# Relus and squares shared out among three engines, some weighted sums in two 64-row phases, both order strings new

## The chip, the cores and the metric

The kernel runs on one core of a Trainium2 chip. The metric is the device time of one execution in microseconds; lower is better. TensorE (PE in the profile) does the matmuls, VectorE (DVE), ScalarE (ACT) and GpSimd (POOL) the elementwise work, SyncE (SP) and POOL start most DMAs.

## The reference

Two layers are computed one after the other for 8 batches of 3136 rows with 256 channels.

```python
scores = (1.0 / S) * np.matmul(z, z.transpose(0, 2, 1))       # z: 3136 x 64
x = u * np.matmul(np.maximum(scores, 0.0) ** 2, v)            # u, v: 3136 x 256
proj = x @ w_proj                                             # 256 x 768, three parts x1, x2, x3
x2_conv = np.fft.irfft(np.fft.rfft(x2, axis=1) * np.fft.rfft(filter_fft, axis=0), axis=1)
out = (x1 * x2_conv * x3) @ w_out
```

The first layer is an attention without softmax: every score is cut at zero and squared. The second one multiplies two projections of its input with a circular convolution of the third.

## The kernel before

The score matrix is symmetric, so a block of it that was squared once can serve twice: as it is, and turned. The 3136 columns of a batch go in seven chunks (CHUNKS, five of 512, one of 256, one of 320), and the rows in 25 tiles of 128. A unit is a pair of row tiles against one chunk. For each unit that is scored (512 in all),

- `score_mm` (L1640) multiplies `zT` by `zT` into one of three pairs of PSUM banks, `ps_s`. z has 64 channels, so these matmuls use 64 rows of the array: two run side by side on the two row halves, or four 64x64 ones when spectral work of that form is in the same stretch ("quarters");
- `relu` (L1870) evicts the scores with a Relu on ScalarE into an fp32 buffer `R_t`, of which there are three (L1873);
- `sq` (L1875) squares `R_t` into a bf16 buffer `A_t`, on ScalarE (L1880) or VectorE (L1882, one multiply of `R_t` by itself);
- `mirror` (L1778) sends the blocks that a later chunk can use through a transposing DMA on SP's queue into a mirror buffer `M_t` (L1805);
- `weigh` (L1700) multiplies `A_t` or a mirror block by the rows of v, `v_t`, with 128-row matmuls, and adds up over all tiles in two PSUM banks `ps_o`, one for each half of the 256 channels (dh).

When a chunk's sum is complete, VectorE multiplies it by u into `xT_t` (L1924), and three projections follow. Two of them make the gate (L1196); the third goes through the spectrum: a first transform (`dft1`), a store to and load from DRAM, a second transform out of 64-row matmuls (`forward`), multiplications with the filter's spectrum in bf16 on VectorE (L1288 for the two products, L1292 and L1293 for the sums), the inverse (`inverse`), again through DRAM, and the last transform with the gate (L1382) and the output projection (`add_end`).

POOL in this kernel starts the DMAs that load and cast u, v and z (L614, L633), and once a chunk copies one element of `xT_t` (L623, `tick`) so as to start them when the chunk is done.

Nothing of this is written in the order in which it runs. Each piece is a `Task` with dependencies, the buffers it takes and frees, and a cost for each engine that may do it. `Plan.go` (L350) goes through time and hands out the tasks; the order in which it does so is the order of each engine's instructions. Two strings steer it. ORDER names, letter by letter, what TensorE does next: S a unit's scores, W a unit's weighted sum, Q a group of spectral matmuls, A, B and Z the projections, transforms and ends. ENGINES gives the engine, letter by letter, to each task that more than one could do (a ScalarE, d VectorE, p POOL). The planner counts 0.096 us where TensorE changes between 64-row and 128-row matmuls.

It also knows a weighted sum in two phases (letters "w" and "v", `weigh_rows` at L1683). In the first, the upper 64 rows are added into one accumulator while the lower 64 rows are added into the other; in the second, they change places. Such matmuls have 64 rows, like the scores. Both phases write the same accumulator, from the two row halves, so `by_rows` (L1673) makes TensorE wait for its own last matmul of the other rows there. The string of before has neither letter; `by_rows` is used only for the last half tile of 64 rows (L1681), whose two halves go to the two accumulators.

Of the kernel before, what the change touches and what calls it, by code (L numbers as in the profile page):

```python
# [16 lines left out]
ALU = mybir.AluOpType  # L17
# [32 lines left out]
    "WWWWSSWWWSWBWBWBWSSSWAAWAASSWAAWASSWBBAWWSSSWWWBWBAWWBSSWAWBWAWSSSWWBBWBWBWBBSSABAWWWBWWBWAAASWAWWWA"  # L50
    "BWSSBWABAWSSABWABAQSSWAWQSWAWSQSWWWWABWBWQSWWAASAWAAWWQSSWABAWSSQWAWQQSWWWSSSWWWWWQSSWWAAWAWAWAQSAWB"
    "QSSWAWAWWQSQWWWWWWSWSWQAWAWWWASSWAWAAWSQSWWAWWASQWWSSWWAASSWWAWWAWSSWSSWWSSWWSSWWWWSSWWBWWWABWSSSWAA"
    "WAASSWBAWBSSBWBAWWSSSWWWWWWSSBAWWABWWAAWSSSWBWBBSBBWAAAWASSBWBSAWBWAWSSWBWBWBWWBAWAAWBWBASABASQBWWAA"
    "BWSQSWWWSSQWWWWWWQSSWWAAAWAWAAWQSSWAABWSSQWWABWSSQWWWWSSQWWWSSSWWWAAWWAAWQSQWAAQSWAWWAWSSQWWWSQWWWSW"
    "QSWWWAWWAAAWWASAWSQAWAWWQSWWSSWWAASSWWWWSSSWAWSSSWWWWWWSSWWWSSWWWBWBABWSSSWAWAAASSWAAWAASSWBBWWABWSS"
    "SWWWWWSSBAWWBWWAASSWABWAASSBWBBAWABAWSSSWBWWBWBWWWSSWWAABWASSWAAAWABWSSQWAWWSBWSQSWBBWBWWWBWWSSQWWAA"
    "AWWSQBAWASQAWBWABWSSQWAWBWQSSWWWWSQSWWWSQSWWWAAAWAAWSQSWAAWWQSSWWAWWWSQSWWWWQQSWWWWWAASQAWAWAAQSWAWA"
    "WWWWSSSWWWAAWAWSSSWWAWSSSWWSSWWWWSSSWWWWWBSBWBWWSSSWAWAASSWAAWBASSWABBWBWWSSSWWAWBAWBWSSABWBWAWBABWA"
    "AAWSSSWAWBSSAWBWWBBWBWAWSSSWWWWSSWAWAWAAAWSSSWABBWABWBBAWQSSWWBWWBWSSQWWWQSWAAWWWASAAWQSABWAWSQSWAWQ"
    "SSWWWWWQSSWWWWSQBWAAWWQSAAWAWQSSWASAWWQSSWWWQQSWWWWWSQWAWAWAWAWWAAWSSQWWAAWWQSSWWWWWSSWWSSWWASSWWSSS"  # L60
    "WWWAWWWWWSSWAAWWWSSWABWSSBAWAAWSSSWBBWSAAWAAWWASSWABWWBBWWBWWAWWSSAAWASSAWABWSSSWABWSSSWBBWWABBWWBWA"
    "BWWWSSSWWBAAWWASSAAAWSQSWBBBWSQSWWWBWWWAWBBWAWQSWBAWASSWWAWSQQWAAWSQSWBAAWWQSWWBWABWSQSWWWWSSQWWWAAW"
    "SQAAWQSAWAAWSQSWAWWSSQWWWWSQSWWWQSWWAWAWAWAAWWQSSWAAWWSSSWWWAWWSSAWWAAWSSWAWSSSWWSWWWSSWWWWWSSSWWBWW"
    "BWBAWSSSWAWASSWAAAWAAWSSSWWWWBWWBBWBWBSSWBAAWWSSSWWAABWSSSWBBWAWAWBBWSSWBWBWWSSSWWAAWWBWBAAWSSQWWWQS"
    "BBWWSQSWWBBWWWWSQSWWBAWWZAWSQSWBABWWSQWSSSWABWWQSQWWWWWBWSSSWAWAWAWQSQWAWWSSQWWQSSWWWWSSSWWWZWWZWWQW"
    "AWSQWQSAAWWWWSSSWWWAWWQSSWWWWWSSSWAWWWWWWAWWWZZAAZAAZZBBBZZBBBZZBBZZZZZZQBQBZBBBQQQQQQQQBQQQQQZQZZZZ"
# [3 lines left out]
ENGINES = (  # L70
    "aaddddddddaadddddaaaddddaaddadadadddaadaadaaadaaaadddddddddddaaddadaaadadaddaaadaaadaddaddadaaadddaa"
    "adadaaaaaaaaddadadddadadaddaddaddddddadadadaaaaddadddaaddadadaaadadddaaadddaaaaddadaddddadaddadddada"
    "aaadddaaaaaaaddddddaddadddaaadaaaaaadadaaaaadaadddddadaddaaaaaaddaaaaddddddddddaaadadaaadaaddddaddaa"
    "addaadaadaaadadadaddadaaaaaddddadadaddddadaadaddddaadddaaaaadaddadddddaadaaadaadaaddaadadaaddaddaada"
    "daaddadaadaaadaadaddddadddaddddaaaddaadaddadddddaddadddaaaaddadaaadaaadadaddddddadaddddaaddaddaaddad"
    "daaaaaaaaaaddadaddddaaadadaaaaadadaddaaaadaaaadaaadadadadaaaadadaadadddddadadadadadddaaaaaaddadadadd"
    "dadddaaadaadadadadddaaaaaddddadaddaddddadaaaaddddaaddaaaadaaadadddadaddadddaadaaaadadaaddaadaaaadaaa"
    "daadadaaaaadaaaddddddddddaaaaaddadddadddaddadadadadddaadddaaaaaaaaaadaaaadadddadadadddadaaaddaaaaaad"
    "adadddddddddaaadaadaaaadadaadadadaaddaaaaddaaaaaaaadadddaaaaddadaddddadadadadadadadadadadaaaadaaddaa"
    "dadddadaadaaaaadaadadddadadaddadddadddaadaddadadddddaaadaaaaadaddadaadaaadaadaddddaaadaaadaadaddaaaa"  # L80
    "daaaaaddaddadaadddddadddaddadddaaddaaddddaadaadddaddaaaaaddaaaadaadaddddadaddaaddaaddadddadaddddadad"
    "daaaadadaaaaaaaaaaaadddadadaaadadadddaaddaaaaaadaaddaadddadaadddaddaadddaaaadaaaaaaaadaaaaaaaadaaaaa"
    "daaaaaaaaaaaadadddaaaaa"
)
# [1933 lines left out]
```

## Time and profile before

| what | us |
|---|---|
| median of 3 runs | 977.86 |
| lowest and highest of them | 975.88, 980.27 |
| the profiled execution | 977.09 |
| its span, first to last instruction | 975.3 |
| TensorE busy in the span | 942.9 |
| ScalarE, VectorE, POOL busy | 859.5, 830.5, 201.0 |

The profile is of one execution. A row of a group gives line, engine and operation, what is written from what, then the count, the busy time and the mean duration of one in ns, and the idle time of the engine ahead of them with what ended it. A row of the view in order of time gives the start, the duration of a row of like instructions, and in brackets the idle time ahead. A row of the view by stretches gives the stretch and its length, then for PE, PEld (weight loads), DVE, ACT and POOL the busy time and count, then TensorE's granted clock, the DMAs' busy share and GB/s. A matmul's duration contains the way through the array, so that of one is longer than the time by which the next one follows. The granted clock was 0.997 over the span.

### The profile page before, as it was taken

The page shows a single profiled execution, that of the slowest core. Times are in us where ns is not written, and L with a number is a line of the kernel's source. Part 1 is how long each engine was busy: PE and PEld are TensorE (multiplying, and loading weights), DVE is VectorE, ACT ScalarE, POOL GpSimd, SP SyncE. Part 2 cuts the span into 40 slices and gives each one's busy share as a digit, 9 for nine tenths or more (in the row PEclk, how much of TensorE's full clock was granted, in tenths as well). Part 3 has the DMA queues.
Part 4 walks back from the last instruction along what each step waited for, and adds up shares of the span by engine and source line. Part 5 has one row for each costly group of instructions (what it writes and reads, how often), then busy time and mean ns, then how long its engine had stood idle before and what let it go on. Part 6 is the DMA issues. An engine that isn't in the chain of part 4 may idle for free.

```text
span 975.3 us, 19343 instructions
## 1 busy us (share of the span) xinstructions
PE 942.9 (97%) x6664; PEld 468.5 (48%) x6765; DVE 830.5 (85%) x1492; ACT 859.5 (88%) x1161; POOL 201.0 (21%) x426
## 2 busy tenths in 40 slices
PE   6999999999999999999999999999999999999986
PEld 2344544355544545445444465444545455544654
DVE  8875788999899987898978997799888998889896
ACT  6788898999789999899988999899989999899783
POOL 5142311222012311213111130113201322000031
PEclk9999999999999999999999999999999999999998
DMA  9899899968998788997799997998979977896677
GB/s 156 147 173 176 119 176 159 186 127 152 182 219 176 137 185 179 212 175 151 148 207 189 180 150 173 207 198 155 155 157 206 213 155 152 188 207 143 164 208 241
DMA packets 332403, 170.31 MB, mean 175 GB/s; under 512 B 242598, under 2 KB 307942, under 8 KB 332304
## 3 DMA queue, kind: packets, MB, share of 16 engines
q1 hardware_dynamic: 302496, 132.43, 63.3%
q0 software_dynamic: 29168, 35.13, 24.0%
q10 hardware_dynamic: 640, 1.51, 0.5%
q8 instruction: 53, 0.87, 0.4%
q14 instruction: 46, 0.38, 0.1%
HBM read 90.26 MB, written 53.35 MB: 147 GB/s over the span
## 4 chain that ended last, share of the span: by engine, by line
PE 89%; DVE 4%; ACT 2%; DMA 2%; issue 2%; SPq 0%; ACTq 0%; DVEq 0%
PE ps_o_t L540 51%; PE ps_s L540 36%; ACT R_t L1873 1%; DVE A_t L1882 1%; PE ps_o_t L1681 1%; DMA conv_in_t<-spec 1%; DMA spec_in_t<-spec 1%; DVE yT_t L1382 1%; DMA M2e_t<-A_t 1%; DVE xh L1288 1%; DVE R_t L1288 0%; ACT A_t L1880 0%; DVE gate_t L1196 0%; PE ps_s L543 0%; DVE xT_t L1924 0%
## 5 line engine op out<-in xcount | busy, mean ns | idle before, releaser
L1873 ACT ACTIVATE R_t<-ps_s 128x1024 f32<-128x1024 f32 (+4 forms) x512 | 467.1, 963 | 54.2 <-PE ps_s L540 50.9
L540 PE MATMUL ps_o_t<-A_t,v_t 128*128 128x512 bf16 (+2 forms) x1936 | 441.4, 354 | 10.8 <-issue 4.4
L540 PEld LDWEIGHTS <-v_t 128*128 128x128 bf16 x2706 | 242.8, 98 | 255.2 <-issue 76.9
L1882 DVE TENSOR_TENSOR A_t<-R_t 128x1024 bf16<-128x1024 f32 (+2 forms) x274 | 300.4, 1112 | 30.4 <-ACT R_t L1873 27.1
L1880 ACT ACTIVATE A_t<-R_t 128x1024 bf16<-128x1024 f32 (+4 forms) x222 | 222.3, 1019 | 1.9 <-DMA M2e_t<-A_t 0.9
L540 PE MATMUL ps_s<-zT_t 64*128 64x512 bf16 (+5 forms) x1418 | 161.9, 356 | 1.9 <-DVE zT_t L577 0.5
L623 POOL COPY tick<-xT_t 1x1 bf16<-1x1 bf16 x54 | 14.7, 272 | 688.3 <-DVE xT_t L1924 688.3
L540 PE MATMUL ps_s<-xT_t,wp 128*128 128x512 bf16 (+2 forms) x411 | 104.5, 352 | 1.1 <-DVE gate_t L1196 0.5
L1924 DVE SCALAR_TENSOR_TENSOR xT_t<-ps_o_t,uT_t 128x256 bf16<-128x256 f32 (+2 forms) x224 | 76.0, 382 | 23.1 <-PE ps_o_t L540 18.3
L540 PEld LDWEIGHTS <-zT_t 64*64 64x64 bf16 (+1 forms) x1451 | 50.8, 100 | 91.9 <-issue 77.9
L573 ACT ACTIVATE x_t<-ps_s 128x512 bf16<-128x512 f32 (+2 forms) x126 | 71.8, 587 | 16.5 <-PE ps_s L540 14.7
L1196 DVE TENSOR_TENSOR gate_t<-ps_s,x_t 128x256 bf16<-128x256 f32 (+2 forms) x212 | 71.4, 383 | 17.4 <-PE ps_s L540 12.9
L1288 DVE TENSOR_TENSOR xh<-xh,H 128x1024 bf16<-128x1024 bf16 x120 | 82.1, 684 | 2.7 <-ACT xh L573 1.3
L540 PE MATMUL ps_o_t<-M_t,v_t 128*128 128x512 bf16 (+2 forms) x352 | 81.7, 353 | 0.0
L1382 DVE TENSOR_TENSOR yT_t<-ps_s,gate_t 128x512 bf16<-128x512 f32 (+2 forms) x95 | 57.0, 623 | 12.0 <-PE ps_s L540 11.6
L577 DVE CAST x_t<-ps_s 128x512 bf16<-128x512 f32 (+2 forms) x85 | 52.2, 623 | 12.3 <-PE ps_s L540 6.5
L614 POOL DMA_DIRECT2D un_t<-in_u_dram x112 | 59.9, 557 | 7.6 <-issue 5.7
L540 PEld LDWEIGHTS <-wp 128*128 128x128 bf16 x448 | 41.8, 98 | 39.6 <-issue 7.3
L633 POOL DMA_DIRECT2D v_t<-in_v_dram x112 | 59.4, 555 | 5.2 <-issue 1.9
L540 PE MATMUL ps_s<-wp,xT_t 128*128 128x256 bf16 x396 | 58.0, 273 | 0.2
L540 PE MATMUL ps_s<-wo,yT_t 128*128 128x256 bf16 (+1 forms) x360 | 54.3, 273 | 0.3 <-DVE yT_t L1382 0.2
L577 DVE CAST xh<-ps_s 128x512 bf16<-128x512 f32 x64 | 42.5, 684 | 8.7 <-PE ps_s L540 8.7
(166 smaller groups left out, 871.5 us busy)
## 6 DMA issues: line engine op xcount, KB each, us to landing
out_dram<-ost_t SPq DMA_DIRECT2D x60, 256.0 KB
spec<-s_t SPq DMA_DIRECT2D x96, 128.0 KB
spec_in_t<-spec SPq DMA_DIRECT2D x56, 192.0 KB
spec<-gs_t SPq DMA_DIRECT2D x56, 192.0 KB
v_t<-in_v_dram POOLq DMA_DIRECT2D x80, 128.0 KB, 5.0
un_t<-in_u_dram POOLq DMA_DIRECT2D x80, 128.0 KB, 5.4
conv_in_t<-spec SPq DMA_DIRECT2D x34, 256.0 KB
out_dram<-ost_t SPq DMA_DIRECT2D x18, 128.0 KB
```

The lines of the kernel that those rows point to most:

```text
L540: wrote(nc.tensor.matmul(o, *args, **kw), o)
L573: got = nc.scalar.activation(out_, in_, AF.Copy)
L577: got = nc.vector.tensor_copy(out_, in_)
L614: nc.gpsimd.dma_start(out=t[ds(j * N1, N1), lo - t0 : hi - t0, :], in_=x[:, n2 : n2 + hi - lo, :])
L633: nc.gpsimd.dma_start(out=t[ds(j * N1, N1), ds(v_at(a), (b - a) * D)], in_=r[:, n2 + a - lo : n2 + b - lo, :].rearrange("p t d -> p (t d)"),)
L1196: got = nc.vector.tensor_tensor(g[:, ::-1] if h == 0 else g, p, x, ALU.mult)
L1288: nc.vector.tensor_tensor(x[:, 1 - i], x[:, 0], h, ALU.mult)
L1382: got = nc.vector.tensor_tensor(yb["y"][:, dh, 0:w], p, gates[b, c, dh][:, 0:w], ALU.mult)
L1873: has_read(nc.scalar.activation(blocks(box["R"], n, cw)[:rows], p, AF.Relu), p)
L1880: nc.scalar.activation(a, r, AF.Square)
L1882: nc.vector.tensor_tensor(a, r, r, ALU.mult)
L1924: nc.vector.scalar_tensor_tensor(x, f, inv_s2, ut, ALU.mult, ALU.mult)
```

## The change

The Relu becomes a task for ScalarE or VectorE, the square one for ScalarE, VectorE or POOL (not POOL in the first chunk of the first batch). POOL's squares and VectorE's bf16 instructions of the spectrum and of z's copies (`ports`) are planned so that they do not overlap. ORDER and ENGINES are new as a whole: 2303 letters for 2245 and 1746 for 1223. ORDER now has 58 "w" and 58 "v"; ENGINES has 204 "p". The unit's second phase must come ahead of the last weighted sum of its chunk (`seconds`), a mirror buffer counts each of its uses, and the first chunk's transposes are planned as landing 2 us later.

```diff
+def c_pool(n):
+    return 0.12 + n * 0.00173
...
+        self.port = {"DVE": 0.0, "POOL": 0.0}
...
+        if engine in task.ports:
+            self.port[engine] = end
...
+            if e in task.ports:
+                s = max(s, self.port["POOL" if e == "DVE" else "DVE"])
...
             w_ = on("DVE", lambda mul=mul: mul(0), cost, evs, prio=ZP)
+            w_.ports = ("DVE",)
             w_ = on("DVE", lambda mul=mul: mul(1), cost, [w_], prio=ZP, lat=ZL)
+            w_.ports = ("DVE",)
             z_ = w_ if final else on("DVE", add, 2 * c_dve2(2 * D), [w_], prio=ZP)
+            z_.ports = ("DVE",)
...
+            if k == len(plans[b, c]) - 1:
+                deps += [(x, ISSUED) for x in seconds.get((b, c), ())]
...
-            if last:
-                t.frees.append((made[0], 0))
+            if not last:
+                made[0].holders += 1
+            t.frees.append((made[0], 0))
...
-                [] if made else [m_pool(c, a).slots], moves=0.78 * len(ts) * cw / 512, late=LATE_TURN,
+                [] if made else [m_pool(c, a).slots], moves=0.78 * len(ts) * cw / 512, late=LATE_TURN + 2.0 * (b == c == 0),
...
-            def relu(un=un, rows=rows, n=n, cw=cw, box=box):
+            def relu(e, un=un, rows=rows, n=n, cw=cw, box=box):
                 box["R"] = R_p.tile()
                 p = blocks(live[un], n, cw)[:rows]
-                has_read(nc.scalar.activation(blocks(box["R"], n, cw)[:rows], p, AF.Relu), p)
+                r = blocks(box["R"], n, cw)[:rows]
+                if e == "ACT":
+                    has_read(nc.scalar.activation(r, p, AF.Relu), p)
+                else:
+                    has_read(nc.vector.tensor_single_scalar(r, p, 0.0, ALU.max), p)
...
-                    nc.vector.tensor_tensor(a, r, r, ALU.mult)
+                    (nc.vector if e == "DVE" else nc.gpsimd).tensor_tensor(a, r, r, ALU.mult)
...
-            r_ = on(
-                "ACT", relu, c_act(n * cw), [(st, -sum(costs[i + 1 :]) - extra)], [R_p.slots], prio=0
+            r_ = job(
+                None, relu, both(n * cw), [(st, -sum(costs[i + 1 :]) - extra)], [R_p.slots], prio=0
             )
...
-            how = {"DVE": c_dve(n * cw)} if (b, c) == (0, 0) and k > 1 else {"DVE": c_dve(n * cw), "ACT": c_act(n * cw) + 0.039}
+            how = {"DVE": c_dve(n * cw), "ACT": c_act(n * cw) + 0.039, "POOL": c_pool(n * cw)}
+            if (b, c) == (0, 0):
+                del how["POOL"]
             q_ = job(None, sq, how, [r_], [a_p.slots], prio=1)
+            q_.ports = ("POOL",)
```

More of the change, by code (lines that the diff above doesn't have):

```diff
@@ L50 @@
[L50 to L54, printed above, removed]
@@ new lines @@
+    "WSQSWWAAWWwSSSvwwwQSvSvQWAWAAAWSSvQWAWAWWAWWSQSWWWWSSSwWAWAQwQvQvwwSSSWWQvSvWAAWAAWWQSWAWAAWWSSSWWSQ"
+    "QWWWWwSwQSWAAWAQvvSQWWWAASSWWAWSSAWWSQwSWAvSQAAWWWQSSWAWWAWWWWWSQSWWWAAWWAAWQwSQAWSvSAAWAAAWWWWWSSSW"
+    "WWWSSSwwWASSWSvvwSSvSWWWAWWWBWWAWSSAWBWAWBWASSBWASSwWAAWSSSWBBWBWBWSSvSWBWAAWBWAWBBWAWBAWSSBWBWAABWS"
+    "SWSSWWSSBWBWBWWWAWAAWSSSWWWWAAASAAAWAWBWSSSWQSSWWAAWSQSWWWWAWWAWSSSWWWBBAWQQAAWSQwABBWWQSwwSQvvvQWWA"
+    "WWQSWWWWQSSWWAWASSwQWWSQSWWvQSSWBAWAAWAWBWWAAAWSSAWAWWAASQWAAWWSSWWSQSWWWAWWSQSWAWWWWWSSSWWSwSSWWWAA"
@@ new lines @@
+    "vSSWAWWWBWWWSSSWWWWBABWSSSWABSWAABWSSSWWBABWSSBBWABWABWWWAAAWBWAWSSWWWASSWBAAWBABSwSvSSWWABSSWABWABW"
+    "WAWSSAWBASWBAWWAWAwSSSWBABWQQSWBWAWQQSvWAAWWWSQWAWBSSWBWBAWAAWAWWWSSSWWWQSSWQSWWWWQQSWAWAAWAWAWSAWAW"
+    "QQSWAWWSQSWWSwQSWWABWSvSSWWBWWSQAWWAWWSSWWQSSwWAWAWSSvQSWAAWWAWWAAAWAWWWSSAAWWSSSWWAWAWSSSWWWWAWBWWS"
+    "SSWWBBWWBBAWSwSSvSWWAAWABASSWWBAWBSSWWABWAWWBSSBWAWSSWBWBWBWBSSWABAAWBSSwSWWWvSSAAWWABAWWBSSWBAWWAAW"
+    "SSSWWAWSSAWBABSQWAWWSQAAWWQQAWWWWSSSWWWWABWSSQWAWBAWAAAwQvSSWWWAWSSQWBWAQQWWWSQSWWWAWWQSSwWBAWWSSQWv"
@@ new lines @@
+    "SQWWAWSSWWWAWBWAWWAWAWSSQWAQSWAWWSSWAAWWQSSWWAAWWAWAWSSSwwwSSvvvSWWWSSAAWWWWWWASSWWWBAWSSSWWABAWAASS"
+    "WAASSWBBAWSSABWBWBWWBWBAWWAABWWWWSSSWBBWBWSSSWWBABWSSSWBAWBWASSWWWAWSSBWWWBWWSSSWABAWASwQvSQWAWABWAW"
+    "WWSSWAABWWAAAWWSQWAAWBWWSSSWABQwSQABWAAWSSQvWWAWWSSSWWAAWQQWWWWSQSWWSSWWAASQWSwQABWBWAWvQSQWWWWQSAWW"
+    "WWWAWSQWSSSWWWWWAAWAWSQWSSWWAWAWAWSSAAAWwSSSWAAWWSSvSWWWAAWSSWBAWWWBWWSSwSWBAWBWAASvSAAWSSSWWSSWABWW"
+    "AWAWBSSWWBBBWSSBWWWAAWSSSWBABWBBAWSABAWASSWAABWWWBAWBWWWAWWBAWAWSSSwWSSvQWWQSSWWAWWBAAWAWQSQWAWBWWBW"
@@ L68 @@
+    "BBB"
 )
 ENGINES = (
[L71 to L75, printed above, removed]
@@ L84 @@
+    "dddadadddaadadadaddapddapdpaaadadadadaaapdadadaaadddaapdaadapadapdpdpaaadaaadapaddaaaadaddpapdaaadaa"
+    "aapapaaaadpapdaadaaaaaaapapaadaadaaaaaddpaaddddaaaaapapaaaaaddpaaadapaadaaaddaadpadaddaddaaadadddaaa"
+    "adaaddddadaaddaadaaaaaaaaaadaadapdaapaaapdaapapaaaaaaaadaaaapdpaaapaadadadpaaddaaadaadaaaapddddapdda"
+    "papdaaddaapaadpaaaaapadaadaaaaadadpapaaapdddaaaapaaaaaadpaadpapapdadadadpaddddadaaadadpaaaadaaadaaad"
+    "aaaaaaaadaaadaaaaaaaaaaaddaaaadaaaaadadddaaada"
 )
@@ L1544, in go_z @@
                 d = on("DVE", dup, c_dve2(P * (t1 - t0)), [a], [zd_p.slots], prio=2)
+                d.ports = ("DVE",)
                 d.frees.append((a, 0))
@@ L1697, in weigh_rows @@
                     )
-    w_first, w_last = {}, {}
+    w_first, w_last, seconds = {}, {}, {}
     def weigh(un, dhs):
```

49 lines of the change are left out of this document (23 added, 26 removed).

## The prediction

> **What bounds the kernel now.** I read the busy line and the chain on the page first, then the busy time by stretches, then the rows of TensorE in order of time, then the groups.
>
> ```profile
> PE 942.9 (97%) x6664; PEld 468.5 (48%) x6765; DVE 830.5 (85%) x1492; ACT 859.5 (88%) x1161; POOL 201.0 (21%) x426
> ...
> PE 89%; DVE 4%; ACT 2%; DMA 2%; issue 2%; SPq 0%; ACTq 0%; DVEq 0%
> ```
>
> ```profile
> 0.00:30.00 30.00, 21.75 (x110) 8.13 (x112) 23.34 (x57) 20.84 (x28) 13.27 (x35) 1.00 1.10 161
> ...
> 400.00:500.00 100.00, 98.68 (x703) 48.70 (x714) 85.94 (x153) 93.73 (x125) 19.94 (x41) 1.00 0.87 168
> ...
> 940.00:975.30 35.30, 24.70 (x274) 15.74 (x267) 25.94 (x55) 17.74 (x35) 8.02 (x15) 0.92 0.75 224
> ```
>
> TensorE is busy for 98.7 of 100 us in the middle and holds 89% of the chain; it idles only in the first 30 us (8.3) and the last 35 (10.6). So a microsecond of gain must come out of TensorE's own stream or out of the two ends, and any wait put into that stream is paid in full. What that stream wastes is seen where it changes between 128-row matmuls and the 64-row ones of the scores and spectra:
>
> ```profile
> 452.57 1.04 PE L540 MATMUL ps_o_t<-A_t,v_t 128*128 128x256 bf16 x8
> 453.54 0.41 PE L540 MATMUL ps_s<-xh,TZ 64*64 64x512 bf16 x4
> 453.78 0.31 PE L540 MATMUL ps_s<-zT_t 64*64 64x320 bf16 x4
> 454.02 0.83 PE L540 MATMUL ps_o_t<-A_t,v_t 128*128 128x256 bf16 x6
> ...
> 464.47 0.99 PE L540 MATMUL ps_o_t<-A_t,v_t 128*128 128x320 bf16 x6
> 465.39 0.61 PE L540 MATMUL ps_s<-zT_t 64*128 64x512 bf16 x4
> 465.93 1.47 PE L540 MATMUL ps_o_t<-A_t,v_t 128*128 128x512 bf16 x5
> ...
> 467.46 0.59 PE L540 MATMUL ps_o_t<-A_t,v_t 128*128 128x512 bf16 x2
> ...
> 468.65 1.03 PE L540 MATMUL ps_o_t<-A_t,v_t 128*128 128x512 bf16 x4
> ```
>
> Two more 512-column matmuls take 0.44 us (x4 against x2), so one occupies 0.22 us, and by columns one of 256 takes 0.11 and one of 320 takes 0.135. Eight of 256 from 452.57 end at 453.45. Four 64x64 matmuls run side by side, so the next two rows are 0.22 + 0.135 of work; the stretch to 454.02 is 1.45 us for 1.23 of work. The 64-row stretch costs 0.22 us beyond its work. The second one: 1.46 us from 464.47 to 465.93, for 6 x 0.135 + 2 x 0.22 = 1.25 (two matmuls of 64x128 run side by side), 0.21 over. I take 0.215 us a stretch.
>
> **The change, part by part.** Counts are from the instruction order of the two built kernels. Durations are of the profiled execution, 977.09 us: a span of 975.3 and 1.8 around it, and 0.8 under the median of the three runs shown.
>
> *Order of TensorE.* Before, the 64-row matmuls lie in 275 stretches; after, in 248, since 58 of 928 weighted sums now run in two 64-row phases ("w", "v") inside a stretch of scores. Columns streamed stay the same. 27 x 0.215 = **-5.8 us**. The phases bring 427 more matmuls and weight loads; weight loads are 48% busy beside the matmuls, so I cost them at nothing. New is a wait of TensorE for itself, 70 times, when the rows change on the same accumulator. In the order, 54 of them have over 0.5 us of other matmuls in between and are covered; the other 16 have one or two steps of 0.22 us. No such wait is in the trace: between nothing and one such step, 0 to 16 x 0.22 = 3.5; I take **+1.5**, nearer to the middle, as nothing else is queued that could hide them.
>
> *The first 35 us.* A mirrored block's transpose is planned 2 us later for the first chunk.
>
> ```profile
> 29.60 1.23 DVE L1882 TENSOR_TENSOR A_t<-R_t 128x1024 bf16<-128x1024 f32 x1 [2.29 <-DMA M2e_t<-A_t]
> ...
> 31.63 0.59 PE L540 MATMUL ps_o_t<-A_t,v_t 128*128 128x512 bf16 x2 [1.96 <-DVE xT_t L1924]
> ```
>
> VectorE stood 2.29 us for that transpose, and TensorE then 1.96. Between 0 and -2.0; I take **-1.0**, since the same transposes still have to land.
>
> *Who does the elementwise work.*
>
> ```profile
> L1873 ACT ACTIVATE R_t<-ps_s 128x1024 f32<-128x1024 f32 (+4 forms) x512 | 467.1, 963 | 54.2 <-PE ps_s L540 50.9
> ...
> L1882 DVE TENSOR_TENSOR A_t<-R_t 128x1024 bf16<-128x1024 f32 (+2 forms) x274 | 300.4, 1112 | 30.4 <-ACT R_t L1873 27.1
> L1880 ACT ACTIVATE A_t<-R_t 128x1024 bf16<-128x1024 f32 (+4 forms) x222 | 222.3, 1019 | 1.9 <-DMA M2e_t<-A_t 0.9
> ...
> L573 ACT ACTIVATE x_t<-ps_s 128x512 bf16<-128x512 f32 (+2 forms) x126 | 71.8, 587 | 16.5 <-PE ps_s L540 14.7
> ...
> L577 DVE CAST x_t<-ps_s 128x512 bf16<-128x512 f32 (+2 forms) x85 | 52.2, 623 | 12.3 <-PE ps_s L540 6.5
> ```
>
> ScalarE loses 178 Relus (x 0.91, 467.1/512) and 23 squares (x 1.00), and gains 43 evictions (x 0.59): -162 - 23 + 25 = -160 us, to about 700. VectorE loses 181 squares (x 1.10) and 43 evictions (x 0.62), and gains 178 Relus. A Relu on VectorE is not in the trace; the nearest rows, its casts out of PSUM, go at 623 ns for half the size, so 1.1 to 1.25; with 1.1: -199 - 27 + 196 = -30, to 800. POOL gains 204 squares of 949 elements on average. These are not in the trace either; the nearest rows:
>
> ```profile
> L889 POOL MEMSET S<- 128x512 f32 x1 | 0.6, 592 | 0.0
> ...
> masks.py:199 POOL TENSOR_SCALAR_AFFINE_SELECT yT_t<-yT_t 128x128 f32<-128x128 f32 x1 | 0.3, 292 | 0.1
> ```
>
> A pure write goes at 592/512 = 1.16 ns an element, a one-input operation at up to 292/128 = 2.3; a square of 1024 so takes 1.2 to 2.4 us, and twice the one-input time, 4.7, if both inputs are fetched in turn. I take 1.9, between the two rows and nearer to the upper one, which reads as well as writes: 204 x 0.93 x 1.9 = 360 us, POOL at 560 of 975. All three engines have room, so none becomes the bound. But the relief itself buys nothing: TensorE hardly waits for them now, and the longest waits between these engines run the other way (ScalarE's Relus 50.9 us for TensorE, above).
>
> The Trainium skill, "GPSIMD Engine Reference", section 3.1, gives 4497 ns for a two-input operation over 2048 elements; an estimate from that page is 2.25 us for 1024, by which POOL would have 626 us and the sum below some 2 us more. No run here shows it yet.
>
> *What the planner does not see.* It now keeps POOL's squares apart from VectorE's bf16 spectral multiplies, but not from VectorE's squares of fp32, of which 105 remain. The trace has a small probe for that, POOL's one-element copy:
>
> ```profile
> L623 POOL COPY tick<-xT_t x54: 176/177/1238, 33.1 to 903.1; 1x1 bf16<-1x1 bf16 x54
> ```
>
> ```profile
> 466.55 1.21 DVE L1882 TENSOR_TENSOR As_t<-R_t 128x1024 bf16<-128x1024 f32 x1
> 466.57 1.24 POOL L623 COPY tick<-xT_t 1x1 bf16<-1x1 bf16 x1 [7.18 <-DVE xT_t L1924]
> ```
>
> ```profile
> 485.17 0.18 POOL L623 COPY tick<-xT_t 1x1 bf16<-1x1 bf16 x1 [16.39 <-DVE xT_t L1924]
> ...
> 485.29 1.21 DVE L1882 TENSOR_TENSOR A_t<-R_t 128x1024 bf16<-128x1024 f32 x1
> ```
>
> Started 0.02 us after a VectorE square, the copy takes 1.24 us and ends with it; started before one, 0.18. So the two shut each other out for a whole instruction. In the changed order, 28 VectorE squares follow a POOL square that, by the VectorE work in between, would still run (20 us left in all at 1.9); 21 POOL squares come straight after a VectorE square (18 us); 10 come straight after one of the spectral operations, and where POOL slips in between two of these, VectorE stands 1.9 us: 19. That is up to 57 us of waiting on two engines. Behind a waiting VectorE are its PSUM evictions, and TensorE's next write to that bank waits for them; behind a waiting POOL square is the fp32 buffer, one of three, which the next Relu needs. TensorE pays between nothing and all 57. I take a quarter, **+14**: the ends of these waits are spread, VectorE's 15-18% of idle time makes up many, but three PSUM pairs leave no room for a whole 1.9 us.
>
> The Trainium skill, "SBUF — State Buffer", section "Who interferes with whom", says the same of a VectorE instruction with two SBUF inputs and a GpSimd one that reads SBUF, in both directions. The 1.24 us copy agrees for POOL's side; no run here shows VectorE waiting, and if it did not, a quarter of 18 would remain and the sum be 976.
>
> *POOL's DMAs.* The same 348 are issued, now behind squares, so some 2 us later and more.
>
> ```profile
> v_t<-in_v_dram POOLq DMA_DIRECT2D x80, 128.0 KB, 5.0
> ```
>
> They land 5.0 us after issue, and the next chunk is 18.6 us away (485.17 - 466.57): hidden, as long as delays stay under 13 us.
>
> Sum: 977.1 - 5.8 + 1.5 - 1.0 + 14 = 985.8, so **986 us**.
>
> **Rivals.** *The plan holds* (other side): the shut-outs fall into idle time of VectorE and POOL, and only the stream counts: 977.1 - 5.8 - 2.0 = 969. For it: VectorE 800 and ScalarE 700 of 975, and before, TensorE waits for neither. Against: it needs nearly every one of some 59 meetings to be absorbed. From its 969, up to 4 us of waiting may be passed on before the kernel is no longer faster by over 0.5%.
> *Gain and loss cancel*: a tenth of the 57, 977.1 - 5.8 + 1.5 - 1.0 + 5.7 = 977.5.
> *POOL too slow*: at 4.7 us a square, 204 x 0.93 x 4.7 + 201 = 1093 us is more than the span, and POOL is the bound: 1093 at least. Against: one-input 2.3 is itself mostly fixed cost on 128 elements. At 2.4, POOL has 656 and is no bound.
> *The change does nothing*: excluded, the built order has the 204 POOL squares and 178 VectorE Relus.
>
> **How the numbers follow.** Forecast, with 11 to 30 us passed on (977.1 - 5.3 + 11 to 30), 983 to 1002: 0.47. Plan holds, 965 to 972.9: 0.33. Cancel, 973 to 982.7: 0.17. POOL too slow: 0.03. The range leaves out the last and the outer ends: 966 to 1002; the forecast's own range is 983 to 1002. Within 0.5% (4.9 us) of 977.9 a measurement of this kernel can't tell a change from none: faster 0.33, same 0.17, slower 0.50.
>
> **What would show it.** Right: POOL squares whose durations come in two kinds, about 1.9 us and longer by up to 1.2 beside VectorE squares; VectorE's multiplies and squares longer than 0.68 and 1.21; TensorE idle in the middle stretches rising from 1.3 to 2.5-3 us in 100, with VectorE or POOL as releaser. Wrong: TensorE at 98.7 or more of every 100 us in the middle, which would be the plan holding. Stretches of 64 rows still costing more than 0.215 with the two phases inside would move the loss to the stream itself. What I doubt most is the quarter.

## The result and the profile after

| what | before | after |
|---|---|---|
| median of 4 runs each, us | 978.06 | 1040.17 |
| lowest and highest | 975.88, 980.27 | 1036.73, 1043.12 |
| profiled execution, its span | 977.09, 975.3 | 1038.8, 1037.0 |

The ratio is 1.0641 (95%: 1.0616 to 1.0666): 62 us slower, where 8 were forecast and the range ended at 1002. The busy line and the chain of the kernel after, from its page:

```profile
PE 966.8 (93%) x7192; PEld 477.3 (46%) x7192; DVE 883.8 (85%) x1446; ACT 725.4 (70%) x1003; POOL 578.1 (56%) x630
...
PE 65%; DVE 16%; issue 7%; DMA 4%; ACT 4%; POOL 2%; SPq 1%; ACTq 0%; DVEq 0%; POOLq 0%
```

ScalarE fell by 134 us and POOL rose by 377 (160 and 360 were worked out). VectorE was to fall by 30 and rose by 53, and it now has 16% of the chain, for 4% before. TensorE's count differs by more than the 427 new matmuls because about a hundred matmul records are missing from the trace of before (6664 matmuls for 6765 weight loads); I use no difference of these busy times. The view by stretches shows the middle (columns as before):

```profile
100.00:200.00 100.00, 97.70 (x821) 47.68 (x820) 87.07 (x137) 76.22 (x106) 61.99 (x64) 1.00 0.88 152
...
400.00:500.00 100.00, 95.38 (x712) 47.25 (x712) 87.61 (x144) 74.64 (x107) 56.12 (x63) 0.98 0.94 162
500.00:600.00 100.00, 90.94 (x617) 41.40 (x614) 83.40 (x121) 63.57 (x84) 63.24 (x57) 0.98 0.81 166
```

Between 100 and 1000 us TensorE is idle for 2.1 to 9.1 us of every 100, where it was 1.3 in the stretch shown of before, and in four of these nine stretches the granted clock is 0.98. The groups of one shape each say whose work became longer: VectorE's before, then POOL's and VectorE's after.

```profile
L1882 DVE TENSOR_TENSOR A_t<-R_t 128x1024 bf16<-128x1024 f32 x208 | 251.3, 1218 | 21.9 <-ACT R_t L1873 18.6 <-DMA M2e_t<-A_t 2.3
...
L1288 DVE TENSOR_TENSOR xh<-xh,H 128x1024 bf16<-128x1024 bf16 x120 | 82.1, 684 | 2.7 <-ACT xh L573 1.3
...
L1292 DVE TENSOR_TENSOR xh<-xh 128x512 bf16<-128x512 bf16 x56 | 23.8, 424 | 1.8
L1293 DVE TENSOR_TENSOR xh<-xh 128x512 bf16<-128x512 bf16 x56 | 23.4, 418 | 0.0
```

```profile
L1910 POOL TENSOR_TENSOR A_t<-R_t 128x1024 bf16<-128x1024 f32 x159 | 314.9, 1995 | 245.6 <-ACT R_t L1899 149.4 <-DVE R_t L1901 75.5 <-issue 11.4
```

```profile
L1901 DVE TENSOR_SCALAR R_t<-ps_s 128x1024 f32<-128x1024 f32 x137 | 165.4, 1219 | 39.3 <-PE ps_s L556 22.8 <-issue 8.5 <-POOL A_t L1910 5.2
L1910 DVE TENSOR_TENSOR A_t<-R_t 128x1024 bf16<-128x1024 f32 x80 | 124.2, 1560 | 10.1 <-ACT R_t L1899 9.2
L1304 DVE TENSOR_TENSOR xh<-xh,H 128x1024 bf16<-128x1024 bf16 x120 | 104.3, 874 | 2.0 <-ACT xh L589 1.0
...
L1308 DVE TENSOR_TENSOR xh<-xh 128x512 bf16<-128x512 bf16 x56 | 30.1, 537 | 1.8
...
L1309 DVE TENSOR_TENSOR xh<-xh 128x512 bf16<-128x512 bf16 x56 | 29.0, 517 | 0.0
```

The Relu on VectorE reads PSUM and stays at 1219 ns. All four groups with two SBUF inputs grew: the square (L1910, before L1882) from 1218 to 1560 ns, the gate's multiply (L1304, before L1288) from 684 to 874, its sums from 424 and 418 to 537 and 517. Row by row, 26 of the 105 squares waited 30.3 us together and 26 of the 240 multiplies and sums 34.9 us; the rest took their usual time. Each that waited ends a fixed time after the end of a POOL square: a square of 1024 about 1.08 us after it, a multiply 0.55, a sum 0.28. On POOL, the square's median over all tiles of 1024 is 1893 ns, and 47 of 167 are longer, by 16 us in all. The longest of the waits, in order of time:

```profile
557.30 6.61 DVE L1304 TENSOR_TENSOR xh<-xh,H 128x1024 bf16<-128x1024 bf16 x1
557.69 5.67 POOL L1910 TENSOR_TENSOR A_t<-R_t 128x1024 bf16<-128x1024 f32 x3
...
559.08 1.03 PE L556 MATMUL ps_o_t<-M_t,v_t 128*128 128x512 bf16 x4
...
564.63 0.68 DVE L593 CAST gs_t<-ps_s 128x512 bf16<-128x512 f32 x1
565.36 0.42 PE L556 MATMUL ps_s<-T,conv_in_t 128*128 128x128 bf16 x3 [5.26 <-DVE gs_t L593]
```

A multiply of 0.68 us took 6.61: three POOL squares in a row ran first. Behind it on VectorE stood an eviction, `gs_t`, and TensorE waited 5.26 us for that bank: the path of the loss in five rows. Just afterwards the clock falls:

```profile
557.00:564.90 7.90, 3.11 (x22) 1.23 (x15) 7.87 (x5) 3.03 (x4) 6.36 (x5) 1.00 0.60 116
564.90:568.60 3.70, 3.24 (x11) 1.28 (x11) 1.99 (x5) 0.00 (x0) 0.00 (x0) 0.54 0.54 145
568.60:572.00 3.40, 3.40 (x39) 1.52 (x38) 1.88 (x4) 3.00 (x5) 0.00 (x0) 1.00 0.89 187
```

For 3.4 us TensorE ran at about half clock. The trace has five such spells before the last 10 us, each at the end of a stall; before had none there.

The sum over TensorE: from the starts of successive matmuls, less the time of their columns and 0.25 us for a change between 64 and 128 rows, gaps of over 0.3 us add up to 65.0 us, for 12.3 before: +53. (The first expectation below has 71 and 57, since there a matmul that runs beside others is counted with a half or a quarter of its columns.) Five spells at half speed cost 5 x 3.4 / 2 = 8.5. The 27 saved stretches give 5.8 back, by the price of the prediction. That makes +55 of the 61.7 us between the two spans; where the other 6 lie is not shown.

### The profile page after: what moved, and what is told of

Same layout as the page of the kernel before. It is cut to its first block, busy times and chain, and to the rows that moved or that the text cites. A ratio compares the mean times of both kernels' runs of the same rounds, so it can differ in the third digit from the quotient of the medians.

```text
span 1037.0 us, 20464 instructions
## 1 busy us (share of the span) xinstructions
PE 966.8 (93%) x7192; PEld 477.3 (46%) x7192; DVE 883.8 (85%) x1446; ACT 725.4 (70%) x1003; POOL 578.1 (56%) x630
## 4 chain that ended last, share of the span: by engine, by line
PE 65%; DVE 16%; issue 7%; DMA 4%; ACT 4%; POOL 2%; SPq 1%; ACTq 0%; DVEq 0%; POOLq 0%
PE ps_o_t L556 34%; PE ps_s L556 27%; PE ps_o_t L1701 4%; DVE xh L1304 3%; DVE R_t L1901 3%; DVE A_t L1910 3%; ACT R_t L1899 2%; POOL A_t L1910 2%; DVE xT_t L1955 1%; DVE xh L1309 1%; DMA conv_in_t<-spec 1%; DMA spec_in_t<-spec 1%; DVE xh L593 1%; DVE yT_t L1401 1%; DMA out_dram<-ost_t 1%
## 5 line engine op out<-in xcount | busy, mean ns | idle before, releaser
L1910 POOL TENSOR_TENSOR A_t<-R_t 128x1024 bf16<-128x1024 f32 (+2 forms) x196 | 362.6, 1866 | 280.4 <-ACT R_t L1899 163.7
L556 PE MATMUL ps_o_t<-A_t,v_t 128*128 128x512 bf16 (+2 forms) x1824 | 427.3, 359 | 2.7 <-DVE A_t L1910 1.9
L1899 ACT ACTIVATE R_t<-ps_s 128x1024 f32<-128x1024 f32 (+3 forms) x334 | 310.9, 957 | 126.6 <-PE ps_s L556 97.0
L556 PEld LDWEIGHTS <-v_t 128*128 128x128 bf16 x2462 | 221.1, 98 | 242.6 <-issue 76.8
L1901 DVE TENSOR_SCALAR R_t<-ps_s 128x1024 f32<-128x1024 f32 (+4 forms) x178 | 197.4, 1120 | 47.3 <-PE ps_s L556 25.6
L1908 ACT ACTIVATE A_t<-R_t 128x1024 bf16<-128x1024 f32 (+4 forms) x197 | 191.1, 982 | 16.7 <-DVE R_t L1901 14.8
L1910 DVE TENSOR_TENSOR A_t<-R_t 128x1024 bf16<-128x1024 f32 (+2 forms) x103 | 144.7, 1413 | 12.0 <-ACT R_t L1899 10.8
L1304 DVE TENSOR_TENSOR xh<-xh,H 128x1024 bf16<-128x1024 bf16 x120 | 104.3, 874 | 2.0 <-ACT xh L589 1.0
L556 PEld LDWEIGHTS <-zT_t 64*128 64x128 bf16 (+1 forms) x1426 | 53.9, 100 | 103.6 <-issue 83.6
L589 ACT ACTIVATE s_t<-ps_s 128x512 bf16<-128x512 f32 (+1 forms) x73 | 42.1, 586 | 25.5 <-PE ps_s L556 17.7
```

The source lines that it names most:

```text
L556: wrote(nc.tensor.matmul(o, *args, **kw), o)
L589: got = nc.scalar.activation(out_, in_, AF.Copy)
L1304: nc.vector.tensor_tensor(x[:, 1 - i], x[:, 0], h, ALU.mult)
L1899: has_read(nc.scalar.activation(r, p, AF.Relu), p)
L1901: has_read(nc.vector.tensor_single_scalar(r, p, 0.0, ALU.max), p)
L1908: nc.scalar.activation(a, r, AF.Square)
```

## The experiments

**Theory**: POOL's squares and VectorE's two-input instructions keep each other waiting, and practically all of it reaches TensorE. **Rivals**: (A) the new order with its two phases is too tight, or costs by itself; (B) POOL's 1.9 us a square and its queue make results late. All times are medians; "before" ran beside each (977.1 to 980.4 us), so two runs with different such neighbours can be compared to 2 or 3 us.

### Taking the collisions away, and putting them into the kernel before

No square on POOL, its letters turned into ScalarE's:

```diff
-    "aaddddddddaadaadaaadadaadadadadaddaaadddaadaaadadadadadadadaaadadadadaadaaaapaadadpaaaadpddapdaddadd"
+    "aaddddddddaadaadaaadadaadadadadaddaaadddaadaaadadadadadadadaaadadadadaadaaaaaaadadaaaaadaddaadaddadd"
...
```

> The kernel after with its 204 POOL squares moved to ScalarE; letters of the order string, the two-phase sums and everything else stay. Theory (the 57 us of new TensorE stalls come from POOL's squares and VectorE's two-input instructions keeping each other waiting): with no square on POOL the gate's multiply goes back from 874 to about 684 ns and VectorE's 1024-element squares from 1560 to about 1220 ns; TensorE's stalls over 0.3 us fall from 71 us to 15 to 25 us, and the time to 970 to 990 us. ScalarE takes on some 200 squares of about 1 us and goes from 725 to about 910 us busy, which may itself cost up to 15 us. Rival A (the new order of TensorE's stretches with its two-phase sums is itself too tight): the time stays above 1015 us although the multiplies are short again. Rival B (POOL's 1.9 us for a square make its results late, with or without VectorE's waits): the time falls as under the theory, so this run does not tell B from the theory; the next one does.

Measured: 1016.4 us, ratio 1.0389 (1.0351 to 1.0428). Multiply and square are back at 685 and 1219 ns, as expected, but the time falls by 24 us only. ScalarE is busy for 885 us, and TensorE's largest sum of waits is for ScalarE's Relus (7.5 us in 21). Inconclusive: the letters were chosen with POOL in mind, and this moves 159 us of work (884.5 less 725.4) to another engine.

POOL busy as long, but reading one element:

```diff
-                    (nc.vector if e == "DVE" else nc.gpsimd).tensor_tensor(a, r, r, ALU.mult)
+                        nc.gpsimd.tensor_copy(A[0:1, 0:1], R2[0:1, 0:1])
+                        nc.gpsimd.memset(A[:rows, 0:w_], 0.001)
+                        nc.gpsimd.memset(A[:rows, 0 : w_ // 2], 0.002)
+                        nc.gpsimd.tensor_copy(A[0:1, 0:1], R2[0:1, 0:1])
```

> The kernel after, but each POOL square is replaced by a one-element copy, a fill of the whole tile, a fill of half of it and a second one-element copy: POOL is busy about as long and releases the buffers about as late, but reads next to nothing. What is left out: the squares of those 204 units, so the output is not the reference's. Theory (it is POOL reading while VectorE reads two operands that makes both wait): VectorE's multiplies and squares go back to about 684 and 1220 ns and the time falls to 965 to 990 us, if the fills take about 1.9 us together. Rival B (POOL's duration and queue alone make the results late): the time stays at 1020 to 1040 us with short multiplies. If the fills too keep VectorE waiting, the multiplies stay near 870 ns and the time near 1040 us, and then reading is not what matters.

Measured: 986.3 us, ratio 1.0078 (1.0044 to 1.0111). The groups of this run, VectorE and then POOL:

```profile
L1911 DVE TENSOR_TENSOR A_t<-R_t 128x1024 bf16<-128x1024 f32 x80 | 96.9, 1219 | 12.1 <-ACT R_t L1899 9.5 <-DMA M2e_t<-A_t 2.0
L1304 DVE TENSOR_TENSOR xh<-xh,H 128x1024 bf16<-128x1024 bf16 x120 | 81.5, 684 | 2.4 <-ACT xh L589 1.7
```

```profile
L1916 POOL MEMSET A_t<- 128x1024 bf16 x159 | 151.6, 953 | 9.4
L1917 POOL MEMSET A_t<- 128x512 bf16 x159 | 83.8, 527 | 9.1
```

POOL has 571 us, as in the kernel after (578), and VectorE no longer waits. 54 of the 62 us are gone, with ORDER, ENGINES and phases untouched. Rival A is out as the main cause, and so is B.

The kernel before, with 204 squares on POOL that nobody needs:

```diff
+                if (b, c) != (0, 0) and count[0] * 204 // 490 > (count[0] - 1) * 204 // 490 and count[1] < 204:
+                    nc.gpsimd.tensor_copy(tick2[:], A[0:1, 0:1])
+                    x = ident[:, 0:64].unsqueeze(1).to_broadcast([P, 15, 64])
+                    nc.gpsimd.tensor_tensor(idle_out[:].rearrange("p (i j) -> p i j", j=64), x, x, ALU.mult)
```

> The kernel before with 204 squares of 960 elements added on POOL, spread over the whole run, into a tile that nothing reads, so that nobody waits for their results; the order of all other work is that of before (the pool of transposed inputs has 7 buffers instead of 8 to make room). Theory: VectorE's gate multiplies and squares grow as in the kernel after (684 to 800 to 900 ns, 1218 to 1350 to 1550 ns) and TensorE is late for it: 1005 to 1045 us, since before leaves TensorE no more slack than after does. Rival A or B (order, phases or POOL's late results): nothing depends on these squares, so the time stays at 976 to 984 us.

Its control, two fills in place of each idle square:

```diff
-                    nc.gpsimd.tensor_tensor(idle_out[:].rearrange("p (i j) -> p i j", j=64), x, x, ALU.mult)
+                    nc.gpsimd.memset(idle_out[:], 0.001)
+                    nc.gpsimd.memset(idle_out[:], 0.002)
```

> The control of the run with idle squares: the kernel before with the same 204 places on POOL, but two fills of 960 elements each instead of a square, about as long in all and reading one element. Theory (only a POOL instruction that reads SBUF makes VectorE wait): 976 to 985 us, VectorE's multiplies and squares at 684 and 1218 ns. Rival (any busy POOL, or the 8th buffer taken away, or the one-element copies cost the time): over 1010 us.

Measured: 1129.5 us, ratio 1.1553 (1.1508 to 1.1597), with squares; 991.0, ratio 1.0109 (1.0063 to 1.0154), with fills. The groups with squares, then with fills:

```profile
L1885 DVE TENSOR_TENSOR A_t<-R_t 128x1024 bf16<-128x1024 f32 x208 | 344.8, 1672 | 7.4 <-ACT R_t L1876 6.1 <-POOL idle_out L1892 0.7
L1291 DVE TENSOR_TENSOR xh<-xh,H 128x1024 bf16<-128x1024 bf16 x120 | 115.7, 964 | 2.2 <-ACT xh L573 0.5 <-DVE zd_t L1534 0.2
```

```profile
L1885 DVE TENSOR_TENSOR A_t<-R_t 128x1024 bf16<-128x1024 f32 x208 | 251.2, 1217 | 21.5 <-ACT R_t L1876 15.0 <-DMA M2e_t<-A_t 2.3 <-DMA M_t<-A_t 1.4
L1291 DVE TENSOR_TENSOR xh<-xh,H 128x1024 bf16<-128x1024 bf16 x120 | 82.0, 683 | 2.7 <-ACT xh L573 1.1 <-DVE zd_t L1534 0.2
```

Squares that nobody waits for cost 138 us over fills, far more than expected, as VectorE has 286 squares here, not 105: it waits 131 us on them and 43 on the gate. About 0.8 of VectorE's waiting is paid, as in the kernel after (54 of 65). What the control itself costs, 11 us, I have not separated: one buffer fewer, `A_t` held until POOL's copy, or DMAs behind the fills.

No sum in two phases (each "w" a "W", no "v"):

```diff
-    "ASSWASWSWSSWAAwwSSvSSwvSWBWvSSWWSSWWSSWWWWSSWWAWWAWAWSwSSvSWWSSSWWAAWWBBWWWWAWSSSWWWBSSwAWWABBWSAvSw"
+    "ASSWASWSWSSWAAWWSSSSWSWBWSSWWSSWWSSWWWWSSWWAWWAWAWSWSSSWWSSSWWAAWWBBWWWWAWSSSWWWBSSWAWWABBWSASW"
...
```

> The kernel after without a two-phase sum: each such sum is again one group of two stretches; the 204 POOL squares stay. By the prediction's sum the 27 saved stretches are worth 5.8 us and the 70 waits of TensorE for itself cost 1.5 us, so the theory expects 1038 to 1052 us, with VectorE's multiplies as long as in the kernel after (about 870 ns). Rival A (the two-phase sums and the place they take in the order cost the time): 975 to 1015 us.

Measured: 1059.2 us, ratio 1.0820 (1.0762 to 1.0879). The phases are not what costs; without them it is slower still. It is 19 us, not 4; the same edit is made without collisions further down.

### How much is POOL's length, and how the waits add up

Short fills on POOL, every second square real, and a planner that knows of VectorE's squares:

```diff
+                        nc.gpsimd.tensor_copy(A[0:1, 0:1], R2[0:1, 0:1])
+                        nc.gpsimd.memset(A[:rows, 0 : n * cw].bitcast(F32), 0.001)
```

> The kernel after, with each POOL square replaced by a one-element copy and one fill of the tile as 32-bit words, some 0.6 us instead of 1.9, that reads one element only (left out: the squares of those 204 units, so the output is not the reference's). The run with two fills of 1.4 us together gave 986.3 us with VectorE's times back to normal, 9 us above the kernel before; this one asks where those and the missing 5.8 us of saved stretches went. Theory: POOL's length makes those results late, so short fills give 965 to 975 us. Rival: the new order of TensorE's work is by itself too tight, whatever POOL does: 982 to 990 us.

```diff
+                    count[0] += e == "POOL"
+                    if e == "POOL" and count[0] % 2:
+                        nc.gpsimd.tensor_tensor(a, r, r, ALU.mult)
...
```

> The kernel after, where every second POOL square is left as it is and the other is the two fills of the earlier run (left out: the squares of 102 units, so the output is not the reference's). Theory (VectorE's waits pass to TensorE in proportion, with no slack that takes up the first of them): the middle between 986 and 1040, so 1005 to 1022 us, with the gate's multiply near 780 ns. Rival (the prediction's idea that a first part of the waits is taken up by slack and only the rest is paid): less than a third of the 54 us, 988 to 1002 us.

```diff
-            q_.ports = ("POOL",)
+            q_.ports = ("POOL", "DVE")
```

> The kernel after, with one word more in its planner: VectorE's squares too are planned as excluding POOL's (in the kernel after only VectorE's bf16 multiplies are). Both strings stay, so each engine has the same instructions; only their order on VectorE, ScalarE and POOL changes. Theory (the waits themselves cost the time, in any order): 1020 to 1050 us, VectorE's multiplies and squares still near 850 and 1500 ns. Rival (the order is wrong only because the planner did not know of the squares' waits): below 1005 us.

Measured: 977.6 us, ratio 0.9983 (0.9957 to 1.0009), with short fills; 1006.7, ratio 1.0269 (1.0240 to 1.0299), with every second; 1050.9, ratio 1.0712 (1.0680 to 1.0744), with the planner told.

So POOL's length is worth 9 us (986.3 less 977.6), and the time with short fills lies between the two ranges expected. The first half of the squares' reading costs 20 us (VectorE's waits are halved too, 32.8 us), the second 34: there is no free first half, as the rival had it. Telling the planner made it 11 us slower than the kernel after, just above the theory's 1050, although VectorE waits less: its waits on squares fell to 14.4 us (the mean of 1024 elements to 1388 ns, not the 1500 expected), those on the gate stayed at 35. So the new order costs something else, which this run does not show; TensorE has 28 more weight loads there, so its own stream changed as well. And even with POOL free and no collision, the new strings give 978, not the 969 of "the plan holds". The waits of TensorE in the run with short fills:

```profile
PE ps_s L556 <- DMA conv_in_t<-spec: 7.9, 4, 3.8
```

Four times the last transform, the one ahead of the gate, comes before the loads of what the inverse stored have landed; no such wait is among the longer ones of before. That is more than the 5.8 us that the stretches save, and the likely reason why nothing is left of them; it was not tested apart.

### Which of VectorE's instructions, and whether it must be POOL

The gate's multiplies and sums as fills, so that only squares can collide; then VectorE's squares as fills, twice:

```diff
-                nc.vector.tensor_tensor(x[:, 1 - i], x[:, 0], h, ALU.mult)
+                nc.vector.tensor_copy(x[0:1, 1 - i, 0, 0, 0:1], x[0:1, 0, 1, 1, 0:1])
+                nc.vector.memset(x[:, 1 - i].bitcast(F32), 0.001 * (i + 1))
...
```

> The other half: the kernel after with all squares as they are, but the gate's multiplies and sums on VectorE replaced by fills of about their length (0.6 and 0.3 us, with a one-element copy; left out: the gate in the transformed domain, so the output is not the reference's). Only VectorE's squares can then collide with POOL's. Theory: 54 x 34/64 = 29 us less than the kernel after, 1006 to 1018 us. Rival A (the multiplies carry nearly all): 986 to 998 us. Rival B (the squares carry nearly all): 1028 to 1040 us.

```diff
+                        nc.vector.tensor_copy(A[0:1, 0:1], R2[0:1, 0:1])
+                        nc.vector.memset(A[:rows, 0:w_].rearrange("p (i j) -> p j i", i=2), 0.001)
+                        nc.vector.tensor_copy(A[0:1, 0:1], R2[0:1, 0:1])
```

> The kernel after, POOL's 204 squares kept, but VectorE's 103 squares replaced by fills of about 1.2 us that read one element (left out: the squares of those units, so the output is not the reference's). Only VectorE's bf16 multiplies and sums of the gate can then collide with POOL. In the kernel after VectorE's excess is 30 us on its squares (80 x 0.34 and 19 x 0.16) and 34 us on the multiplies and sums (120 x 0.19 and 112 x 0.11); all reading collisions together are worth 54 us. Theory (each wait counts alike): 54 x 30/64 = 25 us less than the kernel after, 1010 to 1022 us. Rival A (the gate's multiplies stand nearer to TensorE's next stretch and carry nearly all): 1028 to 1040 us. Rival B (the squares carry nearly all): 990 to 1003 us.

```diff
-                        nc.vector.memset(A[:rows, 0:w_].rearrange("p (i j) -> p j i", i=2), 0.001)
+                        nc.vector.memset(words, 0.001)
+                        nc.vector.memset(words, 0.002)
```

> The run with fills in place of VectorE's 103 squares once more, as two fills of whole 32-bit words in one piece (0.49 us each for 1024 elements in the run with the gate's fills, with the two one-element copies about 1.2 us) instead of one strided fill, before which VectorE stood still for 3.7 us each time (left out: the squares of those units, so the output is not the reference's). POOL's squares can now meet only the gate's multiplies and sums. The complement, with only VectorE's squares left to meet them, came out 21.6 us below the kernel after, of 54 us for both. Theory (the waits add up): 54 - 21.6 = 32 us below, 1002 to 1014 us. Rival A (waits of either sort suffice to make TensorE late, so taking one sort away gives less): 1016 to 1030 us. Rival B (the squares were nearly all): below 998 us.

Measured: 1018.6 us, ratio 1.0412 (1.0388 to 1.0436), without the gate's collisions; 1394.3 with strided fills for the squares; 1034.4, ratio 1.0576 (1.0536 to 1.0616), with whole words. The strided fill is a failed edit:

```profile
L1916 DVE MEMSET A_t<- 128x1024 bf16 x80 | 73.0, 912 | 300.0 <-issue 300.0
```

VectorE stood still 3.75 us ahead of each, for a reason I did not look for. The second one is flawed as well: from the first copy to the last it takes 1.63 us, for 1.22 of a square, 44 us more VectorE time in all. The run without the gate's collisions has the same flaw to a lesser degree: with its copy a fill takes 0.79 us for a multiply of 0.68, and 0.54 and 0.48 for sums of 0.42, some 24 us more VectorE time in all. So the gate's collisions cost 22 us or more, and the squares' share stays open between 6 us and 32.

The two phases without collisions (short fills, and no "w" and "v"):

> The run with POOL's short fills (977.6 us), with no sum in two phases, so that no collision and no late POOL lies over the difference (left out: the squares of POOL's 204 units, so the output is not the reference's). By the prediction's price the phases save 27 stretches x 0.215 = 5.8 us and cost 1.5: theory 980 to 987 us. Rival (the engines' letters and the place of every stretch were chosen together with the phases, so taking them out loses far more than the stretches): over 995 us; then the run says nothing on the price of the phases alone.

Measured: 1002.7 us, ratio 1.0254 (1.0209 to 1.0300). That is the rival: the letters belong together, and the run says nothing on the phases' own price. The loss is not in stalls: TensorE's idle time adds up to 27.1 us there, and to 31.8 in the run with short fills and the phases. The 19 us of the same edit with collisions say as little on the price.

Last, VectorE's waits made by hand, in the kernel with two fills (986.3 us): an idle load ahead of an instruction, which starts when its input is there.

```diff
+        n = fills[what].get(met[what], 0)
+        met[what] += 1
+        if n:
+            nc.vector.tensor_copy(idle_e[:, 0:1], x)
+        for _ in range(n):
+            nc.vector.memset(idle_d[:], 0.0)
```

> The run with two fills in place of each POOL square (986.3 us, no collision), with a small idle load ahead of every gate multiply (a one-element copy and a fill, about 0.19 us), sum (a copy, 0.1 us) and square (a copy and two fills, 0.29 us) of VectorE, each started by the instruction's own input: as much VectorE time in all as the collisions of the kernel after cost it, 55 to 65 us, but spread evenly (left out: the squares of POOL's units). Theory (the order bears small delays; lumps break it): 988 to 1003 us. Rival (VectorE has no time to spare at all): 1025 to 1045 us.

> The same collision-free kernel, with an idle load of about 1.25 us ahead of every 9th of the gate's multiplies and sums and every 4th square of VectorE, about 52 in all and 65 us: like the kernel after in number and length, but at other places and without a wait on POOL. Theory (lumps break the order wherever they fall): 1020 to 1045 us, TensorE's stalls over 0.3 us at 55 to 75 us in all. Rival A (it matters where the collisions fall, or POOL's own waits): 995 to 1015 us. If the even load costs as much as this, VectorE's time itself is short.

> The collision-free run with two fills in place of each POOL square (986.3 us), with an idle load ahead of the same 52 VectorE instructions that waited for POOL in the traced run of the kernel after, each as long as that wait (0.09 us and 0.167 us per further fill, as measured in the run with lumps): 35.3 us on 26 multiplies and sums and 30.3 us on 26 squares, the longest 5.9 us (left out: the squares of POOL's units). POOL itself never waits here. Theory (VectorE's waits are the cause, in full): 1022 to 1042 us. Rival (POOL's own waits for VectorE, some 20 us, and what they make late are half of it): 1000 to 1018 us.

> The same 52 idle loads with the same lengths, but at other instructions: each half the list of its sort further on, so that none falls where a collision fell. If long waits break the order wherever they fall: within 10 us of the run that plays them back in place. If it matters where they fall (collisions come where VectorE, ScalarE and POOL are all pressed, close ahead of TensorE's next need): at least 15 us less than that run.

| idle load of VectorE | in all, us | time, us | ratio (95%) |
|---|---|---|---|
| a little ahead of each, 345 times 0.12 us | 40 | 994.3 | 1.0164 (1.0144 to 1.0185) |
| 52 lumps of 0.78 us | 41 | 1000.6 | 1.0231 (1.0207 to 1.0255) |
| the 52 waits of the kernel after, in place | 66.5 | 1037.0 | 1.0594 (1.0541 to 1.0648) |
| the same, elsewhere | 66.5 | 1032.8 | 1.0555 (1.0497 to 1.0613) |

A load is counted from the start of its copy to the start of the instruction that it holds up. The first two were lighter than the 55 to 65 us meant, since the fills run into the next instruction; so the even load does not settle whether VectorE has time to spare for all of it, though 40 us of it cost only 8. A lump is seen in these rows of the second run, 0.77 us from the copy to the multiply that it holds up:

```profile
315.22 0.14 DVE L686 COPY idle_e<-xh 1x1 bf16<-1x1 bf16 x1
315.31 0.76 DVE L688 MEMSET idle_d<- 128x40 f32 x5
315.99 0.65 DVE L1315 TENSOR_TENSOR xh<-xh,H 128x1024 bf16<-128x1024 bf16 x1
```

The third settles it: with fills on POOL that read one element each, VectorE's own 52 waits put back by hand make the time of the kernel after, whose ratio, 1.0641, lies within this run's interval. TensorE then waits as it did there, 5.2 us at the same eviction:

```profile
PE ps_s L556 <- DVE gs_t L593: 6.3, 4, 5.2
```

And it does not matter much where they fall: elsewhere they cost 4 us less, within the spread of the runs.

How steep it is with length: if half a microsecond of each wait is absorbed and the rest paid, 52 lumps of 0.78 us cost 52 x 0.28 = 15 us, and 14 were measured (1000.6 less 986.3). The 52 played back cost 42, to which come some 8 us of half clock (24.8 us of it in that trace, 8.9 in the one with fills). That makes 50, and 51 were measured. The half microsecond is an estimate fitted to these two runs, not a value of its own. Two runs that it was not fitted to come out near it: with every second square 18.6 us of VectorE's waits lie over half a microsecond, with 4.6 of half clock 23, for 20 measured; with the idle squares 110, with 18 of half clock 128, for 138.

## Why the prediction was wrong

- **The order of TensorE, -5.8: right in size.** The median stretch without a stall still costs 0.213 us (64x128 form) and 0.239 (64x64), for 0.212 and 0.235 before. Of the 1.5 us for TensorE's waits for itself nothing is seen: in the kernel after, all groups of matmuls of L1701, the two phases, have 0.0 us of idle time ahead of them; only weight loads of that line waited for such matmuls, 1.4 us in 4. That the new order would meet late loads (7.9 us) was in no part of the sum.
- **The first 35 us, -1.0:** the 2 us stall at 29.3 us is absent from the run with short fills; in the kernel after, one of 1.54 us comes at 35.5 us in its place.
- **POOL's square at 1.9 us: right,** 1.89 alone, and as foretold in two kinds, the longer ones of up to 3.47 us. By the 4497 ns for 2048 elements of the Trainium skill, "GPSIMD Engine Reference", section 3.1, an estimate is 2.25; this trace has less. That POOL is no bound was right; that its length costs nothing was not (9 us).
- **The collisions, 57 us: right in kind, somewhat low.** Forecast were 28 VectorE squares with 20 us, 10 waits at the gate with 19, and 21 POOL squares with 18. The trace has 26 with 30.3, 26 with 34.9, and 47 with 16. At the gate the planner keeps the two apart on paper only: a plan of start times does not bind engines that run as soon as their inputs are there.
- **"TensorE pays between nothing and all 57. I take a quarter, +14": the step that failed.** It paid 54 us for the reading alone (1040.2 less 986.3), over 0.8 of VectorE's 65. The text argued from shares of idle time: VectorE's 15 to 18% would make up many waits. But a wait of 1.26 us on average does not use idle time elsewhere in the span; it has to fit into the slack at its own place, and the runs with lumps put that at some half a microsecond. The prediction had said what speaks for this, "three PSUM pairs leave no room for a whole 1.9 us", and yet took a quarter. At 0.8 of its own 57 the sum would have been 977.1 - 5.3 + 46 = 1018. The rest is sizes: VectorE's part of the 57 was 39 us and came out at 65, POOL's length cost 9 that the sum put at nothing, and the late loads took back the stretches. From the runs, 977.6 with short fills, 9 for POOL's length and 54 for its reading make the 1040.
- **The rule on the shared ports.** The Trainium skill, "SBUF — State Buffer", section "Who interferes with whom", has both directions, and that a GpSimd instruction that only writes does not collide. The runs now show both: VectorE's multiply takes 874 ns beside squares and 684 beside fills. That whichever starts first goes first, and the other waits for that one instruction, as the prediction's probe suggested, is not the whole of it. A waiting multiply was passed by three squares in a row; and the multiply that starts at 582.98 us, 0.84 us ahead of any POOL square, longer than its own 0.68, still ended only after the next square. In both cases POOL was busy issuing DMAs when the multiply started; why it waited then is not shown.
- **Rivals:** "the plan holds" (969) is refuted even without collisions: 978. "Cancel" and "POOL too slow" did not happen.

## What to carry to other kernels

When work goes to GpSimd that reads SBUF, list every VectorE instruction with two SBUF inputs and count the meetings; where TensorE follows a fixed order at 98% busy, price each wait at its length less some slack (about half a microsecond here), and not by the average idle time of VectorE. Test it ahead of a rewrite with idle squares in the old kernel, against idle fills as a control: here they told 138 us in one run. And a planner that keeps two engines apart by planned times does not keep them apart in fact.

## What the hardware did that was not expected

- One waiting VectorE multiply was overtaken by three POOL squares in a row: 6.61 us for 0.68.
- TensorE's clock halves for 3.4 us after single stalls of 2.8 to 5.4 us (from 45.7, 445.0, 559.9 and 981.2 us), and once after one of 1.6 us with another of 0.8 close behind (from 214.7); after another one of 2.8 us (from 584.3) it did not. The Trainium skill, "TensorE: Matmul & The Clock Gate", section "Why this matters for your kernels", asks for no gaps above about 3 us; the one of 1.6 us is below that. So length alone does not decide. The spells begin at 49.8, 217.0, 449.1, 565.2 and 985.0 us, which are 49, 68, 34 and 123 times 3.413 us apart, and in all other traces with several spells they are whole multiples of it apart too. What goes with them is TensorE's work in the 3.41 us of that grid just before, taken from the matmuls' starts and columns: over the 18 traces, 94 of 95 such stretches at full clock with less than 0.36 of work are followed by half clock, 18 of 57 with 0.36 to 0.45, and none of 5025 with more. The stall of 1.6 us made one with 0.357; that from 584.3 us was split over two, the emptier with 0.55.
- A strided 2-byte fill on VectorE, after a one-element copy, left the engine still for 3.75 us; the same bytes as 32-bit words in one piece left 0.17.
